# A parallel attention and gated block, forward and backward, on one core: another layout of the weight loads, paired query weights, wider products and a new order

## The chip, the core and the metric

The kernel runs on one core of a Trainium2 chip. A core has five engines with an instruction stream each: TensorE (PE, with PEld for its weight loads), VectorE (DVE), ScalarE (ACT), GpSimd (POOL) and SyncE (SP). Sixteen DMA engines move data between HBM and the core's SBUF; nearly every transfer here is issued from SP. The metric is the device time of one execution in microseconds (us), and lower is better.

## The reference, cut to what matters

The reference takes one decode step for two sequences (B = 2, one query position, D = 576) and returns the output and all eight gradients.

```python
xn = _layernorm(x)                                    # (2, 1, 576)
out = x + A(xn, k_cache, v_cache, wq, wo) + Bm(xn, w_gate, w_up, w_down)

# A: 32 query heads over 16 K/V heads, 4096 cached positions of 128 numbers each
q = (xn @ wq) per head;  k, v = repeat(k_cache, 2), repeat(v_cache, 2)
p = softmax(q @ k.T * 128 ** -0.5);   A = (p @ v) @ wo
# Bm: F = 4608
h = (xn @ w_gate) * (xn @ w_up);      Bm = h @ w_down

out, vjp = jax.vjp(f, x, k_cache, v_cache, wq, wo, w_gate, w_up, w_down)
return out, *vjp(grad_out)
```

Each cache has 2 x 16 heads of 4096 x 128 bf16, 1 MB a head. The gradients of the caches and of the five weight matrices are outer products of a few rows, but they are as large as the tensors themselves: the profile counts 92.48 MB read from HBM and 92.48 MB written.

## The kernel before, in words

The work on the caches is cut into 16 steps `s`. A step has one sequence `b = s % 2` and one group `g = s // 2` of two K/V heads, hence four query heads. A step loads two K heads and two V heads (`load_kv`, L1117, 1 MB each), turns them in 32 x 32 blocks on DVE (`turn`, the helper `t32` at L464), forms scores (`score`, L1234), the softmax, the scores' gradient, the weighted sums (`contract`, L1407), and then the gradients of K and V (`head_outer`, L1255) in PSUM. ACT or DVE (`cp`, L468 and L470) copies those to SBUF, and `put` (L691) stores 1 MB a head.

A group also needs four heads' columns of `wq` and rows of `wo` (`load_w`, L1132 to L1141). `group_front` forms the queries from `wq` (L966) and takes the gradient back through `wo`; `group_back` forms the output's share and the input's gradient, for which it turns the group's `wq` on DVE (L464, tile `ww`). The gated block goes in nine parts of 512 columns of F (`mlp`), loaded two at a time: 1024 columns of `w_gate` and `w_up` (L1155 the first 512 rows, L1158 the last 64, the tail), and two parts of `w_down` (L1164). The gradients of `wq`, `w_gate` and `w_up` are stored for up to four parts at once (`wide_outer`, products at L759), those of the tails apart (`tail_outer`).

How the rows of a weight matrix lie in SBUF matters here. Of the first 512 rows, partition `p` holds rows `p`, `p + 128`, `p + 256` and `p + 384`; the loads and the loops over `dc` in `group_front`, `mlp` and `dxn` follow that.

The order of the work is not written by hand. While the program is built, `Order.run` plays all streams (`turn`, `fronts`, `attend`, `backs` and so on) against a model of engine times, DMA lines and buffers. Priorities come from `pr` and the tables `HEAD`, `TAIL`, `PR`, `OFF`; `MLP_AT`, `WQ_AT`, `WO_AT` say after which K/V load a weight load may go. The instructions of each engine are emitted in that order. SP's DMAs are one such list: a store that waits for its copies holds up each load behind it.

Buffers: `NBIG` = 16 buffers of 1 MB are shared by K/V loads (`kv`, up to 7), turned blocks (`X`), gate and up weights (`G`) and stores (`st`, up to 4); 6 `ww` buffers hold `wq`, `wo` and `w_down`; the gradients that `wide_outer` multiplies lie in 5 tiles `D` and 6 tiles `Q`.

Of the kernel before, what the change touches and what calls it, by code (L numbers as in the profile page):

```python
# [13 lines left out]
P = 128  # L14
# [90 lines left out]
class Order:  # L105
# [3 lines left out]
    def __init__(self):  # L109
        self.free = {e: 0.0 for e in ("PE", "ACT", "DVE", "POOL", "SP")}  # L110
        self.slots = {}
        self.home, self.cap, self.used = {}, {}, {}
        self.lines = Lines()
        self.quad, self.kind = (None, 0.0, 0.0), None
        self.streams = []
        self.count = 0
        self.log = []
        self.lanes = {"HW": [], "SW": []}
# [17 lines left out]
    def advance(self, s, value):  # L136
        while True:
# [13 lines left out]
            elif kind == "spawn":  # L151
                self.spawn(s.req[1], s.req[2], s.ready)
            elif kind == "prio":
                s.prio = (s.req[1], s.prio[1])
            elif kind == "lset":
                s.req[1].t = Late(s.land)
            elif kind == "lrel":
                self.pool(s.req[1])[s.req[2]] = s.land
                if s.req[1] in self.used:
                    self.used[s.req[1]] -= 1  # L160
            else:
                return

# [31 lines left out]
    def run(self):  # L195
        while self.streams:
# [8 lines left out]
            if e is not None:  # L205
                t, _, s, e = min((c for c in cand if c[3] == e and c[0] <= t + SLACK[e]), key=lambda c: (c[1], c[0]))
# [27 lines left out]
            elif r[0] == "dma":  # L234
                self.free[e] = t + r[2]
                s.land = self.lines.push(e == "POOL", t + r[2] + LATENCY[e], r[3], r[4])
# [54 lines left out]
def DMA(engine, cost, nbytes, row=8192):  # L291
# [5 lines left out]
NBIG, NGU, NWW, NBD = 16, 1, 6, 3  # L297
CAP = {"kv": 7, "X": 15, "st": 4, "G": 2}
OFF = {"mload": {0: 96.4, 1: -26.1, 2: 880.0, 3: 94.9, 4: -346.4, 5: -156.4, 6: -87.6, 7: 8.9, 8: 146.0, 9: -13.8,
       10: 91.2, 11: -99.0, 12: -61.7, 13: 103.4, 14: 404.9, 15: -150.5}, "wload": {0: -50.8, 1: -238.8, 3: -315.1,  # L300
# [7 lines left out]
       "load": {0: 195.1, 2: 227.9, 3: -17.9, 4: -185.2, 5: -111.1, 6: -195.0, 7: -157.8, 8: 475.0, 10: 90.3,  # L308
       11: -45.9, 12: -113.2, 13: 340.9, 14: 38.7, 15: -10.9}, "front": {1: -351.4, 2: 56.5, 3: 55.5, 4: 1100.6,
       5: 44.1, 6: -364.2, 7: -8.3, 8: -150.0, 10: 278.3, 11: -217.9, 12: 25.9, 14: -46.2, 15: 809.6},  # L310
       "turn0": {0: -96.0, 1: 186.1, 2: 128.2, 3: 344.6, 4: 259.4, 5: 502.5, 6: 22.0, 7: -80.7, 8: 79.6, 9: -81.7,
       10: -397.2, 11: -241.3, 12: -223.5, 13: -195.7, 14: 186.3, 15: 55.8}, "con": {0: -121.6, 1: 346.9, 2: 7.7,
# [3 lines left out]
       "back": {0: 413.0, 1: -6.1, 2: 233.5, 3: 588.7, 4: 263.1, 5: -92.6, 6: -1063.1, 7: 111.3, 8: 44.4, 10: -315.0,  # L316
# [3 lines left out]
       11: -7.4, 12: 14.8, 13: 23.1, 14: 398.8, 15: -591.6}, "dsc": {0: -130.6, 2: -312.2, 3: -339.0, 4: 207.7,  # L320
       5: -530.4, 6: 41.2, 7: 323.6, 8: -0.4, 9: 644.8, 10: -274.2, 11: 125.7, 12: 309.5, 13: -43.5, 14: 192.2,
       15: -0.7}, "mlp": {0: 81.6, 1: -71.7, 2: 147.3, 3: -224.1, 4: -6.3, 5: 14.7, 6: 616.7, 7: -152.4, 8: -159.9,
       9: 42.7, 10: -45.7, 11: 24.0, 12: 245.6, 13: -6.0, 14: -127.2, 15: -22.4}, "att": {0: 251.8, 1: -520.9,
       2: 62.8, 3: 21.5, 4: -199.3, 5: -366.7, 6: 546.7, 7: -109.6, 8: -638.2, 9: 1.5, 10: -174.3, 11: 113.2,
       12: 18.4, 13: -79.6, 14: -31.8, 15: -12.4}, "conv": {1: 208.9, 2: -233.1, 3: 119.4, 4: 0.3, 5: -102.3,
       6: -60.5, 8: 9.6, 9: -114.9, 10: 102.5, 11: 45.1, 12: 165.0, 13: -36.7, 14: 23.6, 15: -54.5}}
MLP_AT = [1.22, 5.43, 16.39, 14.23, 25.87, 33.08, 39.74, 38.29, 101.55]
WQ_AT = [-2, 5, 9, 22, 32, 30, 50, 47]
WO_AT = [-10, -14, -8, 3, 37, 36, 48, 48]
LATENCY, DRY = {"SP": 0.5, "ACT": 0.5, "POOL": 0.57}, 0.4  # L330
LM, LAG = 0.67, 1.7
CLK = 2.0
BIAS = 0.196
SLACK = {"PE": 0, "ACT": 0.21, "DVE": 0.48, "POOL": 937075237.61, "SP": 6210463039.22}
STEP = 28.0
HEAD = {"turn0": -109.2, "turn1": -1091.6, "att": -224.6, "dsc": -208.3, "con": 390.9, "out1": -1503.4,
        "out0": 772.1, "front": 803.5, "back": -715.7, "W0": 1770.6, "W1": 26.3, "BD1": 1384.3, "BD0": 3893.2,
        "conv": -396.6, "load": 469.8}
TAIL = {"turn0": -167.6, "turn1": 1451.8, "att": -1608.9, "dsc": 1030.3, "con": 1577.7, "conv": 3.8, "out1": 2595.4,
        "out0": -474.0, "front": -576.5, "back": 355.2, "W1": 698.1, "BD1": -2114.1, "BD0": 951.5, "load": 618.9,  # L340
        "W0": 381.9}
PR = {"turn0": 410.8, "turn1": -89.2, "att": -1586.1, "dsc": -1566.9, "conv": 32.7, "con": -332.6, "out1": 2476.3,
      "out0": 866.1, "front": 94.3, "back": -196.2, "W0": -1406.3, "W1": -128.9, "BD1": 1706.7, "BD0": -477.7,
      "mlp": -490.2, "wout": -771.6, "store": -4.6, "load": 401.7, "wload": -1959.2, "fin": -1327.7, "const": 3504.2,
      "mload": -416.2}
# [8 lines left out]
def kernel(  # L354
# [45 lines left out]
    WB = 4 * FS + 256  # L400
# [10 lines left out]
    kv_t = X_t = st_t = G_t = tiles("big", NBIG, [P, NCH * Dh])  # L411
# [4 lines left out]
    tl_t = tiles("tl", 2, [P, FS])  # L416
    BD_t = tiles("BD", NBD, [P, 16, Dh])
# [3 lines left out]
    D_t = tiles("D", 5, [P, 2, P])  # L421
# [12 lines left out]
    Q_t = tiles("Q", 6, [P, P])  # L434
# [125 lines left out]
    Emore, Ein, Eprep = Event(), Event(), Event()  # L560
# [19 lines left out]
    def front_y():  # L580
        yield WAIT(Ein)
# [10 lines left out]

    def front():
        xb, yb = xy[:, 0:D], xy[:, D:2 * D]
        for t, src in ((xb, A_x), (yb, grad_out)):
            yield DMA("ACT", 0.45, 2304, 1152)
            nc.scalar.dma_start(t, src.rearrange("b s d -> (b s) d"))
        yield ("lset", Ein)
        yield SPAWN(front_y(), -999.0)
# [11 lines left out]
        nc.vector.tensor_scalar(xnb[:], xb, mv[:, 0:1], rstd[:], op0=ALU.subtract, op1=ALU.mult)  # L611
# [6 lines left out]
        for c in range(4):  # L618
            nc.tensor.transpose(tp[:, 2 * c:2 * c + 2], xnb[:, c * P:(c + 1) * P], ident[0:2, 0:2])
        nc.tensor.transpose(tp[0:64, 8:10], xnb[:, 512:576], ident[0:2, 0:2])  # L620
        nc.tensor.transpose(tp[:, 10:12], xnb[:, 448:576], ident[0:2, 0:2])
# [3 lines left out]
        nc.vector.tensor_copy(xs[64:128, 5, 0:2], tp[64:128, 10:12])  # L625
        yield REL("m", i)
# [8 lines left out]
        yield DVE(0.3)  # L635
        nc.vector.memset(gg[:, 1], 0.0)
# [6 lines left out]
        for a in range(4):  # L643
            for c in range(4):
                nc.tensor.matmul(tp[32 * c:32 * c + 32, 2 * a:2 * a + 2], lhsT=xb[:, P * c + 32 * a:P * c + 32 * a + 32],
                                 rhs=ident[0:2, 0:2], start=True, stop=True)
        for a in range(2):
            nc.tensor.matmul(tp[0:32, 8 + 2 * a:10 + 2 * a], lhsT=xb[:, 512 + 32 * a:544 + 32 * a],
# [12 lines left out]
    def stationaries(i, rep, npos, half, costs):  # L661
# [6 lines left out]
        for h in range(2):  # L668
# [5 lines left out]
    def dxn(dp, i, X, S, pos, xoff, xstep, Xt, St, toff, tpos):  # L674
# [6 lines left out]
        for s in range(St):  # L681
            for q in range(4):
                nc.tensor.matmul(dp[32 * q:32 * q + 32, P:160], lhsT=view(Wt[:], 0, P, 8 * tpos(q, s), [[1, 32]]),
# [875 lines left out]
```

## Time and profile before

| what | value |
|---|---|
| three timed runs | median 477.73 us (476.86 to 479.79) |
| the profiled execution | 480.7 us, its span 478.9 us |
| mean granted TensorE clock | 0.704 |
| DMA | 185.95 MB in 41925 packets, 388 GB/s over the span |
| issues from SP, 1 MB each | 74 stores, 32 K loads, 32 V loads, 4 gate and 4 up loads |
| `wq` loads | 8 of 512 KB, 16 of 32 KB |

The span runs from the first to the last instruction on the core; the profiled execution's own time lies 1.8 us above it. In the profile's page, part 1 gives the busy time of each engine, part 2 cuts the span into 40 equal slices, part 3 lists the DMA queues, and part 5 the groups of equal instructions with busy time and the mean of one. A window of the DMA view gives, for a stretch in us from the span's start, the packets that the 16 DMA engines moved, the MB, and the time that the packets took as a share of 16 engines' time. The records of neighbouring packets overlap a little, so a share can pass 100%.

### The profile page before, as it was taken

What the parts mean: (1) busy time and instruction counts of PE and PEld (TensorE: products, weight loads), DVE (VectorE), ACT (ScalarE), POOL (GpSimd) and SP (SyncE); (2) the same over time, 40 slices, a digit from 0 to 9 for tenths busy, and PEclk for the clock granted to TensorE, in tenths of its full rate; (3) what the DMA queues carried; (4) which work ended last, traced back from release to release, by engine and by line L of the source; (5) the groups of instructions that cost most, each with busy time, mean ns of one, the idle gap of its engine ahead of it and who ended that gap; (6) DMA issues with size and microseconds to landing.
All of it is one profiled execution on the core that took longest, in us unless ns stands there. A gap on an engine that the chain in (4) does not pass through costs nothing.

```text
span 478.9 us, 15380 instructions
## 1 busy us (share of the span) xinstructions
PE 375.8 (78%) x6538; PEld 214.9 (45%) x6538; DVE 369.2 (77%) x708; ACT 335.6 (70%) x507; POOL 152.0 (32%) x208
## 2 busy tenths in 40 slices
PE   1668588989878877768878986599887769898894
PEld 1545353545554534446344453464444424444452
DVE  8788787867867976786956987889677958888781
ACT  3139659966787693833869875399776978897871
POOL 0440074343003643003434530032644556333000
PEclk9979676556766677885567595859656876656876
DMA  8999999999999999999999999999999999999994
GB/s 299 355 405 419 391 402 380 353 377 422 422 400 371 395 365 393 423 414 389 316 399 384 354 402 422 421 413 406 346 414 415 418 419 422 419 417 391 425 369 187
DMA packets 41925, 185.95 MB, mean 388 GB/s; under 512 B 3960, under 2 KB 13440, under 8 KB 25472
## 3 DMA queue, kind: packets, MB, share of 16 engines
q1 hardware_dynamic: 41848, 184.96, 98.3%
q8 instruction: 51, 0.84, 0.7%
q14 instruction: 18, 0.15, 0.1%
q10 hardware_dynamic: 8, 0.00, 0.0%
HBM read 92.48 MB, written 92.48 MB: 386 GB/s over the span
## 4 chain that ended last, share of the span: by engine, by line
DMA 46%; PE 25%; DVE 14%; ACT 8%; issue 3%; SPq 2%; POOL 1%; DVEq 0%; ACTq 0%; POOLq 0%
DMA out_dram<-big 18%; DMA big<-in_A_v_cache_dram 15%; DVE big L464 8%; ACT big L468 7%; PE ps_o L1255 4%; DMA big<-in_A_k_cache_dram 4%; PE ps_m L1234 4%; PE ps_m L1407 4%; PE ps_o L722 3%; DMA gu<-in_B_w_up_dram 3%; DMA ww<-in_A_wo_dram 3%; DMA big<-in_B_w_gate_dram 2%; DVE big L470 2%; PE ps_m L678 1%; PE ps_o L759 1%
## 5 line engine op out<-in xcount | busy, mean ns | idle before, releaser
L468 ACT CAST big<-ps_o 128x1024 bf16<-128x1024 f32 (+2 forms) x310 | 277.6, 958 | 47.6 <-PE ps_o L1255 18.9
L464 DVE STREAM_TRANSPOSE big<-big 128x1024 f32<-128x1024 f32 x146 | 175.9, 1224 | 29.7 <-DMA out_dram<-big 16.2
L1222 POOL TENSOR_TENSOR BD<-vr,mask 128x2048 bf16<-128x2048 bf16 x32 | 115.3, 3603 | 105.4 <-ACT vr L468 49.8
L470 DVE CAST big<-ps_o 128x1024 bf16<-128x1024 f32 (+2 forms) x68 | 74.2, 1093 | 16.4 <-PE ps_o L722 7.4
L1234 PE MATMUL ps_m<-big,W 128*32 128x128 bf16 x2048 | 59.9, 282 | 11.3 <-DVE cr L1359 2.6
L1234 PEld LDWEIGHTS <-W 128*32 128x32 bf16 x2048 | 46.7, 125 | 27.9 <-issue 25.7
L1255 PE MATMUL ps_o<-BD,dd 32*128 32x512 bf16 x256 | 45.8, 480 | 9.9 <-ACT big L468 7.9
L671 POOL COPY wt<-wm 64x128 bf16<-64x128 bf16 (+1 forms) x34 | 8.9, 261 | 138.2 <-DVE wm L664 119.5
L1255 PE MATMUL ps_o<-BD,pp 32*128 32x512 bf16 x256 | 48.2, 520 | 5.5 <-ACT big L468 4.0
L1199 POOL COPY W<-rep 32x16 bf16<-32x16 bf16 x128 | 24.5, 192 | 55.8 <-DVE rep L983 33.6
L464 DVE STREAM_TRANSPOSE big<-ww 128x1152 f32<-128x1152 f32 x25 | 34.0, 1359 | 7.7 <-DMA ww<-in_B_w_down_dram 3.5
L1407 PE MATMUL ps_m<-big,pp 128*32 128x512 bf16 x256 | 30.2, 547 | 3.8 <-DMA big<-in_A_v_cache_dram 3.3
L1255 PEld LDWEIGHTS <-dd 32*128 32x128 bf16 x256 | 12.2, 98 | 32.1 <-issue 27.6
L1407 PE MATMUL ps_m<-big,dd 128*32 128x512 bf16 x256 | 25.8, 491 | 0.4 <-DVE oT L1427 0.2
L1255 PEld LDWEIGHTS <-pp 32*128 32x128 bf16 x256 | 10.4, 97 | 28.1 <-issue 24.2
L872 PE MATMUL ps_m<-big,Wdy 128*128 128x128 bf16 x162 | 15.4, 269 | 4.8 <-DVE rz L1320 3.1
L722 PE MATMUL ps_o<-dyr,hb 32*32 32x288 bf16 x288 | 18.0, 382 | 0.2 <-ACT big L468 0.2
L759 PEld LDWEIGHTS <-xnr 32*128 32x128 bf16 x368 | 12.9, 116 | 10.8 <-issue 9.7
L722 PE MATMUL ps_o<-dyr,R 32*32 32x288 bf16 x256 | 16.2, 378 | 1.3 <-ACT big L468 0.9
L872 PEld LDWEIGHTS <-Wdy 128*128 128x128 bf16 x162 | 13.6, 121 | 6.8 <-issue 6.7
L759 PE MATMUL ps_o<-D,xnr 32*128 32x128 bf16 x256 | 13.0, 276 | 3.9 <-issue 2.2
L1308 ACT COPY mr<-m 1x128 f32<-1x128 f32 x16 | 4.7, 295 | 15.8 <-DVE m L1306 15.6
(205 smaller groups left out, 487.3 us busy)
## 6 DMA issues: line engine op xcount, KB each, us to landing
out_dram<-big SPq DMA_DIRECT2D x74, 1024.0 KB, 12.8
big<-in_A_k_cache_dram SPq DMA_DIRECT2D x32, 1024.0 KB, 12.7
big<-in_A_v_cache_dram SPq DMA_DIRECT2D x32, 1024.0 KB, 13.2
out_dram<-big SPq DMA_DIRECT2D x17, 576.0 KB, 10.7
ww<-in_B_w_down_dram SPq DMA_DIRECT2D x9, 576.0 KB, 13.5
ww<-in_A_wo_dram SPq DMA_DIRECT2D x8, 576.0 KB, 7.3
ww<-in_A_wq_dram SPq DMA_DIRECT2D x8, 512.0 KB, 8.0
big<-in_B_w_gate_dram SPq DMA_DIRECT2D x4, 1024.0 KB, 12.3
```

Source lines behind the costliest of these rows:

```text
L464: nc.vector.transpose(out, in_)
L468: nc.scalar.copy(out, in_)
L470: nc.vector.tensor_copy(out=out, in_=in_)
L671: nc.gpsimd.tensor_copy(view(Wt[:], 64 * h, 64, 0, [[dims[-1][1], n], [1, dims[-1][1]]]), view(Wm[:], 64 * h, 64, off, dims))
L722: nc.tensor.matmul(o[32 * q:32 * q + 32, aa, 0:HD2], lhsT=view(t, 32 * q, 32, 2 * A + aa, [[4, 32]]), rhs=dyr[32 * q:32 * q + 32, k * HD2: ...
L759: nc.tensor.matmul(o[:, aa, j * P:(j + 1) * P], lhsT=xnr[32 * a:32 * a + 32, dc * P:(dc + 1) * P], rhs=rhs(a), start=True, stop=True)
L872: nc.tensor.matmul(dh, lhsT=Wdy[:, e, 2 * k:2 * k + P], rhs=view(X[:], 0, P, 64 * k + e, [[D, FC], [2, 32]]), start=(k == 0 and e == 0), s ...
L1199: nc.gpsimd.tensor_copy(view(W_t[t][w][:], 32 * a, 32, 6 + 8 * a, [[G * WW, 4], [WW, G], [1, 2]]), view(rep_t[grp[g]["qs"]][:], 32 * a, 32 ...
L1222: nc.gpsimd.tensor_tensor(BD_t[i][:], view(vr_t[v][:], 0, P, 0, [[0, 16], [1, Dh]]), view(mask16[:], 0, P, 0, [[1, 16], [0, Dh]]), ALU.mult)
L1234: nc.tensor.matmul(sc[32 * cq:32 * cq + 32, :], lhsT=view(W[:], 0, P, (be * G + l) * WW + 6 - 4 * c2 - 2 * l, [[1, 32]]), rhs=view(X[:], 0 ...
L1255: nc.tensor.matmul(o[:, k, :], lhsT=pr2[32 * c4:32 * c4 + 32, :], rhs=BD[32 * c4:32 * c4 + 32, 8 * l + 4 * h2:8 * l + 4 * h2 + 4, :], star ...
L1407: nc.tensor.matmul(ct[32 * j:32 * j + 32, :], lhsT=view(rT, 0, P, 4 * c + 2 * l, [[1, 32]]), rhs=kv_t[kvS[s][t][l]][:, Dh * c:Dh * (c + 4) ...
```

## The change

- **Rows.** [...] In the loads of `wq`, `w_gate` and `w_up` the 576 rows are now cut in 16 blocks of 36. The first 32 of block `e` go to partitions `8e` to `8e + 7`, four neighbouring rows to each (`main_rows`); its last four are the tail (`tail_rows`). The rest of the program follows: `xn` is permuted the same way (`by_rows`), and so are the views for `final_dx`.
- **Pairs.** `wq` is loaded for two groups at once, except for groups 0 and 1: 1024 columns instead of 512, into one of the big buffers (`wq`, up to 2 of them), with the tail in two tiles `qt`. A buffer is free when both groups have turned their half. `ww` has 4 buffers instead of 6, `NBIG` is 17.
- **Wide products.** The 4 slots of `D` and of `Q` lie in one tile each, so a product of `wide_outer` takes up to 512 columns at once instead of 128 at a time.
- **grad_out first.** Its load goes from ACT's queue to the first place of SP's list.
- **Order.** The tables are new, `st` may take 9 buffers and `X` 8, `head_outer` and `wide_outer` wait for part of the product before them, and two of the model's constants differ (`LM` 0.24 for 0.67, `LAG` 2.75 for 1.7).

```diff
-NBIG, NGU, NWW, NBD = 16, 1, 6, 3
-CAP = {"kv": 7, "X": 15, "st": 4, "G": 2}
+NBIG, NGU, NWW, NBD = 17, 1, 4, 3
+CAP = {"kv": 7, "X": 8, "st": 9, "G": 2, "wq": 2}
...
-LM, LAG = 0.67, 1.7
+LM, LAG = 0.24, 2.75
...
+    def main_rows(A):
+        return A.rearrange("(e r) n -> e r n", e=16)[:, 0:32, :].rearrange("e (j c) n -> e j c n", c=4)
+
+    def tail_rows(A):
+        return A.rearrange("(e r) n -> e r n", e=16)[:, 32:36, :]
...
             if kind == "wq":
-                for h in range(2):
-                    yield DMA("SP", 0.36, 64 * 256 * 2, 512)
-                    nc.sync.dma_start(ww_t[w][64 * h:64 * h + 64, 4 * FS:WB],
-                                      A_wq[512:576, n0 + 256 * h:n0 + 256 * h + 256])
...
+                js = [j] if i < 2 else [0, 1] if j == 0 else []
+                for k in js:
+                    yield DMA("SP", 0.36, 64 * FS * 2, 1024)
+                    nc.sync.dma_start(t[64 * k:64 * k + 64, :], tail_rows(A_wq[:, n0 + FS * (k - j):n0 + FS * (k - j) + FS]))
+                if js:
...
+                    width = FS * len(js)
+                    yield DMA("SP", 0.4, 128 * 4 * width * 2, 2 * width)
+                    nc.sync.dma_start(w[:].rearrange("p (c n) -> p c n", n=2 * FS)[:, :, FS * js[0]:FS * js[0] + width],
+                                      main_rows(A_wq[:, n0:n0 + width]))
...
-                                  Wsrc[0:512, f0:f0 + width].rearrange("(c p) n -> p c n", p=P))
+                                  main_rows(Wsrc[:, f0:f0 + width]))
...
-                nc.sync.dma_start(gu[64 * w:64 * w + 64, 0:width], Wsrc[512:576, f0:f0 + width])
+                nc.sync.dma_start(gu[64 * w:64 * w + 64, 0:width], tail_rows(Wsrc[:, f0:f0 + width]))
...
-            for j, rhs in enumerate(rhss):
-                for aa in range(2):
-                    a = 2 * A + aa
-                    nc.tensor.matmul(o[:, aa, j * P:(j + 1) * P], lhsT=xnr[32 * a:32 * a + 32, dc * P:(dc + 1) * P],
-                                     rhs=rhs(a), start=True, stop=True)
+            for aa in range(2):
+                a = 2 * A + aa
+                nc.tensor.matmul(o[:, aa, 0:n * P], lhsT=xnr[32 * a:32 * a + 32, dc * P:(dc + 1) * P],
+                                 rhs=rhs(a), start=True, stop=True)
...
-        t32(pairs(X[:, 0:WB]), pairs(wq[:]))
-        yield REL("ww", st["wq"])
+        t32(pairs(X[:, 0:4 * FS]).rearrange("p (c n) -> p c n", c=4),
+            pairs(wq[:]).rearrange("p (c n) -> p c n", c=4)[:, :, HFS * j:HFS * (j + 1)])
+        yield DVE(0.4)
+        t32(pairs(X[64 * j:64 * j + 64, 4 * FS:5 * FS]), pairs(wt[64 * j:64 * j + 64, :]))
...
     def front_y():
-        yield WAIT(Ein)
+        yield DMA("SP", 0.36, 2304, 1152)
+        nc.sync.dma_start(xy[:, D:2 * D], grad_out.rearrange("b s d -> (b s) d"))
...
-            nc.vector.tensor_scalar(xnb[:], xb, mv[:, 0:1], rstd[:], op0=ALU.subtract, op1=ALU.mult)
+        for d, r in by_rows(xp, xb):
+            nc.vector.tensor_scalar(d, r, mv[:, 0:1], rstd[:], op0=ALU.subtract, op1=ALU.mult)
```

More of the change, by code (lines that the diff above doesn't have):

```diff
@@ L115, in __init__ @@
         self.streams = []
+        self.last = None
         self.count = 0
@@ L162, in advance, with again, stores @@
                 return
+    def again(self, s, e):
+        return ALT if e == "SP" and self.stores(s) == self.last else 0.0
+    def stores(self, s):
+        return s.gen.__name__ in ("put", "final_out", "final_dx")
     def start(self, s):
@@ L339 @@
[L339 to L345, printed above, removed]
+ALT = 0.0
@@ L667, in stationaries @@
         yield POOL(costs[1])
-        for h in range(2):
+        for h in hs:
             off, dims = half(h)
@@ L1018, in group_front, with free_wq @@
         yield SET(st["Ed"])
+    def free_wq(pair):
+        yield WAIT(*pair["turned"])
+        yield REL("wq", pair["w"])
+        yield REL("qt", pair["t"])
     def group_back(g):
@@ L1167, in load_w @@
                 yield SPAWN(mlp(k, hh, sl, Lgu, Ld, d), pr("mlp", MLP_AT[k] / 4))
+    wqs = [dict(turned=events(2)) for _ in range(NG // 2)]
     def load_ws(items):
@@ L1473, in final_out @@
                                  start=False, stop=True)
-        yield from rows_put(o, 0, out_0)
+        yield from rows_put(o, 0, out_0, [
+            (view(xy[:], 0, 2, 64 * k, [[P, 5 - k], [1, 64]]),
+             o[0:2, k, 0:320 - 64 * k].rearrange("p (k n) -> p k n", k=5 - k)) for k in range(2)])
         yield REL("o", i)
```

237 lines of the change are left out of this document (139 added, 98 removed), and 23 rows, old and new, of the table OFF.

## The prediction

> **What bounds the kernel now.** I read the page's busy times first, then its DMA queues, then the rates of the DMA by slices, then single windows of the DMA view where the rate is low, and last what SP waits for.
>
> ```profile
> PE 375.8 (78%) x6538; PEld 214.9 (45%) x6538; DVE 369.2 (77%) x708; ACT 335.6 (70%) x507; POOL 152.0 (32%) x208
> ...
> DMA  8999999999999999999999999999999999999994
> GB/s 299 355 405 419 391 402 380 353 377 422 422 400 371 395 365 393 423 414 389 316 399 384 354 402 422 421 413 406 346 414 415 418 419 422 419 417 391 425 369 187
> ...
> q1 hardware_dynamic: 41848, 184.96, 98.3%
> ```
>
> No compute engine is above 78% of the span, while the packets of SP's queue took 98.3% of all 16 DMA engines' time. So the DMA is the bound, and the time changes only through three things: the time that packets take, stretches in which the DMA runs dry, and the ends of the span. The slices show the first: the DMA is busy throughout, but it moves 415 to 425 GB/s in good slices and 316 to 371 in others. Most of the poor ones lie where gate and up weights load (slices 2, 8, 15, 23, 24), or `wq` and `wo` (13, 29), as SP's issue times say. Two neighbouring windows of the first of these stretches, 12 to 14 us and 14 to 16 us:
>
> ```profile
> q1 hardware_dynamic: 407, 0.80, 107.4%
> ```
> ```profile
> q1 hardware_dynamic: 288, 0.57, 104.2%
> ```
>
> Both are nearly all 2 KB rows of the gated block's weights. Without the few packets under 512 B, which take under 1% of the time, the first holds 382 of 2 KB and two of 8 KB, the second 276 of 2 KB. An 8 KB packet takes 313 ns (28 to 30 us: 102 in 100.3%). So a 2 KB packet takes (1.074 x 16 x 2000 - 2 x 313) / 382 = 88 ns in the first window and 33,344 / 276 = 121 ns in the second. The first is `w_gate`'s main load, the second begins with its tail and `w_up`. Slow stretches follow at every pair of parts: 308 GB/s in 14 to 20 us, 325 in 95 to 102, 344 in 174 to 184, 346 in 271 to 279, against 399 in 12 to 14.
>
> **The change, part by part.** The sum is made against the profiled execution's 480.7 us (span 478.9, 1.8 around it), which is 3.0 above the median of 477.73; at the end I take 3.0 off.
>
> *Fewer, larger packets.* Groups 2 to 7 load `wq` in three pairs: 6 x 512 = 3072 packets of 1 KB become 1536 of 2 KB. The last window, 476 to 479 us, has 35 packets of 1 KB and 2 small ones in 3.4% of 48,000 ns, 47 ns each. So this saves (3072 x 47 - 1536 x 88) / 16 = 0.6 us. The tails go from 1024 pieces of 512 B to 512 of 1 KB. No window isolates 512 B; if one costs half of 47 ns nothing is saved, if it costs as much 1.5 us. I take 0.3, near the lower end: from 2 KB to 1 KB a packet's time falls from 88 to 47 ns, nearly by half. Sum -0.9.
>
> *Which rows an engine reads.* If all slow stretches ran like 12 to 14 us, they would give back 6 x (1 - 308/399) = 1.4, 7 x (1 - 325/399) = 1.3, 10 x (1 - 344/399) = 1.4 and 8 x (1 - 346/399) = 1.1 us, 5.2 in all. The two stretches of `wq` and `wo`, 145 to 148 us at 276 GB/s and 345 to 349 at 277, would give 3 x 0.25 + 4 x 0.25 = 1.8 against the 370 GB/s of a mix of 1 KB (349) and 4.6 KB rows. The upper bound is 7.0. The lower bound is below nothing: if the new rows made all 4608 packets of gate and up take 121 ns instead of a mean near 100 (92 to 95 us: 512 in 107.0% of 48,000), it would cost 4608 x 21 / 16 = 6.0. Neither end is excluded: `w_gate`'s main load runs at 88 ns with the old rows, so they aren't slow by themselves; the slowness begins when a second block of rows is read beside it. [...] I take a gain of 4.0, nearer to the row of 12 to 14 us.
>
> [...]
>
> *The end.* In 472 to 476 us the queue's share is 28.1%, in 476 to 479 it is 3.4%, in 468 to 472 88.5%:
>
> ```profile
> q1 hardware_dynamic: 319, 0.39, 28.1%
> ```
> ```profile
> q1 hardware_dynamic: 37, 0.04, 3.4%
> ```
>
> 0.46 + 2.88 + 2.90 = 6.2 us of DMA time are lost. From 473 on the rate is 14 to 31 GB/s in most slices, a sixteenth of 420: one engine works off its backlog of the last stores. In the changed order `out_0`, a 1 MB store, `out_1` and two 1 MB stores come last, 2.5 us each at 421 GB/s; before, `out_1` itself is last and waits for the input gradient's chain until 473.8 us. So that chain gets cover. But 10.8 MB stand behind the last weight load instead of 11.8, the chain is still there, and so may the lagging engine be. Bounds -3.0 and +2.5 (the 1 MB less); I take -1.5.
>
> *The start.* `grad_out` is issued ahead of the first K load, which moves from 0.73 us to about 1.2 us; group 0 issues one tail fewer behind it. Before the first packets nothing hides this: +0.4, at least 0. The two strided passes that replace one pass over `xn` (0.42 us on DVE) come before the first queries; the DMA works on loads already issued, so nothing.
>
> *DVE, PE and POOL.* Each group's `wq` is turned in 1.22 us (the 128x1024 row) and 0.42 us (the 128x256 row) instead of 1.36: 8 x 0.28 = 2.3 us of DVE, hidden under the DMA but for the last group, +0.3. `wide_outer` issues 96 products instead of 368; the columns streamed are the same, so PE keeps its time and the 272 weight loads less (12.9 us for 368) come off PEld, which overlaps PE. The 64 extra small products of the tail rows (12.2 us for 416 of them, so 1.9) are on PE at 78%. None of it is on the path as long as the DMA is the bound; if that cover goes, +2 on DVE and PE each.
>
> *Buffers and order.* SP's waits before:
>
> ```profile
> SPq L691 <- ACT big L468: 82.6, 49, 7.7
> SPq L691 <- DVE big L470: 49.9, 17, 6.8
> SPq L1117 <- DMA out_dram<-big: 31.9, 13, 4.8
> ```
>
> SP sits 31.9 us at K/V loads until a store frees their buffer, yet the DMA runs dry only in few slices: 0.95 in 216 to 228 us, 0.90 in 228 to 240, 0.94 in 252 to 264, 0.95 in 456 to 468, together 3.1 us. After, up to two of 17 big buffers hold `wq`, so 15 to 17 are left for the rest where 16 were; queued behind a load that waits is every store. The four fixed slots of `D` make part 4 wait for the products of parts 0 to 3; in the compiled order their stores (four of 2 x 2048 columns) come ahead of part 4's loads, so that wait is free. The new order may lose up to 3.1 less or some 12 more (the second rival). I take no change.
>
> Sum: 480.7 - 0.9 - 4.0 - 1.5 + 0.4 + 0.3 = 475.0; less 3.0 is **472.0 us**.
>
> **Rivals.** *A: the slow stretches stay.* They begin with the tail. A tail goes to 64 partitions before and after, so if its destination and not its rows brings the engines out of step, the largest term goes: 476.0. For it: the old rows ran at 88 ns. Against it: the 1 KB stores of the end, tails from 64 partitions among them, show 47 ns. [...]
>
> *B: slower, for want of a big buffer.* When a pair of `wq` is loaded while the former is still held (three times: groups 2, 4, 6), a K/V load has to wait for a further 1 MB store to drain, 2.5 us, and everything on SP queues behind it. In 227 to 231 us this shows what a gap costs: share 70.5%, 1.2 us. With the wait and the stage behind it each handover would cost up to 4 us, 12 in all: 484. It decides from about 10 us of dry DMA beyond the present 3.1. Against it: `ww` no longer holds `wq`, and `st` may take 9.
>
> *C: all goes well.* Slow stretches gone (-7.0), the end gains 3.0: 480.7 - 0.9 - 7.0 - 3.0 + 0.7 - 3.0 = 467.5, and with dry stretches gone 464.5.
>
> **How the numbers follow.** Forecast 0.42, C 0.18, A 0.28, B 0.12. What can be told from no change is 1%, so 473.0 is the limit of faster, 482.5 of slower. The forecast's own spread (its end term between -3.0 and +2.5) leaves a fifth of it above 473. Faster 0.42 x 0.8 + 0.18 + a little of A = 0.56; slower most of B, 0.10; same 0.34. The range takes in C with dry stretches gone, the forecast and A with its bad end, 464 to 480; B is left out.
>
> **What would show it.** Gate and up windows at 380 GB/s and more (A: still 310 to 345); some 2050 packets fewer in all; a share above 60% until 3 us before the end; the dry slices no deeper than 0.90 (B: slices at 0.8 after the `wq` pairs' loads). I am wrong if the new rows slow the loads themselves, or if the compute behind the last load, not the DMA, sets the end.

## The result, and the profile after

The changed kernel takes **523.7 us** (median of four runs, 521.6 to 525.9) against 477.3 us of the kernel before beside it: a ratio of 1.096, 95% interval 1.090 to 1.102. It is slower by 46 us, where 472.0 was forecast. The profiled execution has a span of 521.1 us, 42.2 more than before. (In one experiment below, Order alone, one of four runs lies over 1.5% above the fastest and is left out of its median and ratio.)

Of the page of the changed kernel, the busy times, the DMA slices and the queue that answer to those shown of before (and the line that counts packets):

```profile
PE 383.1 (74%) x6330; PEld 214.6 (41%) x6330; DVE 381.0 (73%) x722; ACT 330.3 (63%) x505; POOL 150.5 (29%) x200
...
DMA  8999999999999999999899999999999999999576
GB/s 271 239 420 343 415 289 367 220 417 421 390 373 351 418 421 427 250 348 426 351 310 291 382 420 420 416 323 361 418 352 424 346 401 416 420 404 289 208 252 260
DMA packets 39698, 185.91 MB, mean 357 GB/s; under 512 B 3784, under 2 KB 9680, under 8 KB 23248
...
q1 hardware_dynamic: 39628, 184.96, 96.9%
```

The good slices are as good as before, 415 to 427 GB/s. But the poor ones, which lay at 316 to 371, now lie at 220 to 351, with the DMA as busy as ever. And the last four slices, some 52 us, are new: the DMA moves 208 to 289 GB/s there, and in the last three it is no longer busy.

The same two windows as before, 12 to 14 and 14 to 16 us, from the DMA view of the changed kernel (queue, packets, MB, share):

```profile
DMA packets 226, 0.48 MB, mean 238 GB/s; under 512 B 12, under 2 KB 12, under 8 KB 220
...
q1 hardware_dynamic: 226, 0.48, 105.4%
```
```profile
q1 hardware_dynamic: 216, 0.44, 107.0%
```

Of the 226 packets of the first, 12 are tiny, 6 have 8 KB, and 208 have 2 KB, so a 2 KB packet takes about (1.054 x 32,000 - 6 x 313) / 208 = 153 ns; in the second all have 2 KB, 34,240 / 216 = 159 ns. Before it was 88 and 121. The two windows hold 424 packets of 2 KB, fewer than the 512 of `w_gate`'s main load, whose tail is issued behind it: this is the main load alone.

The end, in the windows of the changed kernel (busy times and counts of the engines, granted clock, DMA share, GB/s):

```profile
468.00:480.00 12.00, 5.58 (x92) 3.65 (x81) 5.85 (x14) 2.46 (x8) 0.00 (x0) 0.50 1.06 304
480.00:492.00 12.00, 10.90 (x159) 5.91 (x157) 8.43 (x18) 7.75 (x10) 1.70 (x1) 0.72 0.53 218
492.00:504.00 12.00, 10.87 (x234) 5.82 (x233) 9.83 (x18) 10.13 (x15) 2.70 (x4) 0.72 0.66 240
504.00:516.00 12.00, 8.95 (x110) 4.47 (x108) 8.20 (x18) 8.39 (x11) 0.00 (x0) 0.78 0.60 230
516.00:521.00 5.00, 0.00 (x0) 0.00 (x0) 0.00 (x0) 0.00 (x0) 0.00 (x0) 0.50 0.76 315
```

and in the chain that ended last (start, us, engine, tile and line):

```profile
466.32 11.06 DMA gu<-in_B_w_up_dram
477.42 0.86 PE ps_m L883 x24
479.02 0.46 DVE dd L480
...
505.17 0.98 PE ps_o L1529 x16
507.31 1.22 DVE big L486
510.39 1.63 PE ps_o L1571 x8
...
514.94 1.01 ACT big L484
```

The chain passes through the tail of the last `w_up` load, for 11 us, until 477.4. From there to the last copy its long pieces are compute, on PE, DVE and ACT, with the DMA at 53 to 66%. The windows from 480 on lose 12 x (0.47 + 0.34 + 0.40) + 5 x 0.24 = 15.7 us of DMA time. Before, the last two windows lost 12 x 0.05 + 11 x 0.56 = 6.8:

```profile
456.00:468.00 12.00, 11.16 (x243) 7.70 (x241) 9.32 (x20) 9.19 (x15) 1.04 (x4) 0.72 0.95 373
468.00:479.00 11.00, 3.90 (x52) 2.19 (x42) 1.97 (x10) 1.43 (x2) 0.00 (x0) 0.66 0.44 162
```

There the last load in the chain, a K load, landed at 402.6 us. All behind it was compute too, but the DMA had enough in its queue to stay busy beside it until about 468.

What SP waits for, in the changed kernel:

```profile
SPq L718 <- DVE big L486: 109.9, 39, 12.8
SPq L718 <- ACT big L484: 96.0, 50, 9.9
SPq L1160 <- DMA out_dram<-big: 16.7, 8, 7.2
```

The waits of stores for their copies grew from 132.5 to 205.9 us; those of K/V loads for a free buffer fell from 31.9 to 16.7.

All packet records together close the account. Their durations, summed and divided by 16 engines, are the first column; the second is the time for which fewer than 16 packets are in flight, in the same unit, and the third that for which more than 16 are, since some records overlap. Both are counted from the first packet, 10.5 to 11.2 us ahead of the span, to the last, which ends 1.2 to 1.4 us ahead of the span's end in most runs. Packets plus dry less overlap is that stretch. The rows below the second are the experiments of the next section.

| kernel | packets, us | dry, us | overlap, us | span, us |
|---|---|---|---|---|
| before | 474.6 | 22.8 | 8.9 | 478.9 |
| after | 508.5 | 33.5 | 11.3 | 521.1 |
| after, old rows | 475.7 | 33.7 | 8.6 | 491.4 |
| before, new rows | 512.9 | 22.4 | 12.4 | 513.5 |
| before, 32 blocks of 18 rows | 471.9 | 22.6 | 9.1 | 475.7 |
| before, 128 blocks of 4 rows | 471.6 | 22.7 | 9.0 | 476.1 |
| before, wide products | 470.2 | 23.6 | 8.9 | 475.5 |
| before, one planner constant | 477.6 | 34.0 | 8.5 | 493.4 |
| before, grad_out first | 477.1 | 43.2 | 8.6 | 498.5 |
| after, old rows and old tables | 474.0 | 30.9 | 8.6 | 487.0 |
| after, old rows, no Order | 474.0 | 48.5 | 8.4 | 504.4 |
| after, old rows, kv 8 | 475.7 | 47.6 | 8.7 | 502.8 |

So the 42.2 us of span are 33.9 us of longer packets and 10.7 us of dry DMA, less 2.4 us of more overlap. The experiments take the two apart.

### The profile page after: what moved, and what is told of

The parts are those of the page before. It is cut to its first block, busy times and chain, and to the rows that moved or that the text cites. A ratio compares the mean times of both kernels' runs of the same rounds, so it can differ in the third digit from the quotient of the medians.

```text
span 521.1 us, 14927 instructions
## 1 busy us (share of the span) xinstructions
PE 383.1 (74%) x6330; PEld 214.6 (41%) x6330; DVE 381.0 (73%) x722; ACT 330.3 (63%) x505; POOL 150.5 (29%) x200
## 4 chain that ended last, share of the span: by engine, by line
DMA 48%; PE 27%; DVE 10%; ACT 8%; SPq 3%; issue 3%; POOL 0%; DVEq 0%; ACTq 0%
DMA big<-in_A_v_cache_dram 20%; DMA out_dram<-big 18%; ACT big L484 7%; DMA gu<-in_B_w_up_dram 6%; DVE big L480 6%; PE ps_o L1315 5%; PE ps_m L1467 4%; PE ps_m L1293 3%; PE ps_o L749 3%; DMA ww<-in_A_wo_dram 3%; SPq L1215 2%; PE ps_m L901 2%; DVE big L486 2%; PE ps_m L1031 2%; PE ps_m L705 1%
## 5 line engine op out<-in xcount | busy, mean ns | idle before, releaser
L484 ACT CAST big<-ps_o 128x1024 bf16<-128x1024 f32 (+2 forms) x296 | 266.2, 959 | 54.7 <-PE ps_o L1315 33.6
L480 DVE STREAM_TRANSPOSE big<-big 128x1024 f32<-128x1024 f32 x154 | 185.9, 1224 | 35.2 <-DMA out_dram<-big 12.1
L486 DVE CAST big<-ps_o 128x1024 bf16<-128x1024 f32 (+1 forms) x82 | 89.8, 1096 | 20.5 <-PE ps_o L749 7.1
L698 POOL COPY wt<-wm 64x128 bf16<-64x128 bf16 x26 | 7.4, 286 | 115.3 <-DVE wm L691 114.8
L1258 POOL COPY W<-rep 32x16 bf16<-32x16 bf16 x128 | 24.6, 193 | 41.1 <-DVE rep L1015 34.6
L1467 PE MATMUL ps_m<-big,dd 128*32 128x512 bf16 x256 | 29.1, 545 | 8.1 <-DVE acc L1098 6.3
L480 DVE STREAM_TRANSPOSE big<-ww 128x1152 f32<-128x1152 f32 x17 | 23.2, 1362 | 5.3 <-DMA out_dram<-big 4.1
L1031 PE MATMUL ps_m<-big,Wdy 128*128 128x128 bf16 x144 | 14.9, 284 | 4.7 <-DVE big L480 4.5
L705 PE MATMUL ps_m<-big,wm 128*32 128x128 bf16 x416 | 12.5, 275 | 7.5 <-DVE Dall L908 5.8
L901 PE MATMUL ps_m<-big,Wdy 128*128 128x128 bf16 x162 | 16.6, 283 | 1.7 <-DVE rz L1380 1.2
L484 ACT CAST tl<-ps_o 128x256 bf16<-128x256 f32 (+1 forms) x26 | 9.4, 375 | 12.6 <-PE ps_o L849 12.1
L484 ACT CAST osb<-ps_m 128x512 bf16<-128x512 f32 x15 | 8.8, 588 | 12.7 <-PE ps_m L1467 12.6
## 6 DMA issues: line engine op xcount, KB each, us to landing
big<-in_A_k_cache_dram SPq DMA_DIRECT2D x32, 1024.0 KB, 12.5
out_dram<-big SPq DMA_DIRECT2D x17, 576.0 KB, 10.7
big<-in_B_w_gate_dram SPq DMA_DIRECT2D x4, 1024.0 KB, 19.4
```

The lines of the kernel that those rows point to most:

```text
L480: nc.vector.transpose(out, in_)
L484: nc.scalar.copy(out, in_)
L486: nc.vector.tensor_copy(out=out, in_=in_)
L705: nc.tensor.matmul(dp[32 * q:32 * q + 32, 0:P], lhsT=view(Wm[:], 0, P, 8 * pos(q, s), [[1, 32]]), rhs=view(X, 0, P, xoff(q, s), [[xstep, 4 ...
L901: nc.tensor.matmul(dh, lhsT=Wdy[:, e, 2 * k:2 * k + P], rhs=view(X[:], 0, P, 64 * k + e, [[D, FC], [2, 32]]), start=(k == 0 and e == 0), s ...
L1031: nc.tensor.matmul(dp, lhsT=Wdy[:, e, 2 * k:2 * k + P], rhs=view(X[:], 0, P, 64 * k + e, [[D, GH], [2, 32]]), start=(k == 0 and e == 0), s ...
```

## The experiments

The expectations name the theories as they stood at the time.

### The rows, undone and alone

The changed kernel with the old rows and everything else as changed (the permuted `xn` and the views for `final_dx` go back with them):

```diff
     def main_rows(A):
-        return A.rearrange("(e r) n -> e r n", e=16)[:, 0:32, :].rearrange("e (j c) n -> e j c n", c=4)
+        return A[0:512, :].rearrange("(c p) n -> p c n", p=P)
...
     def tail_rows(A):
-        return A.rearrange("(e r) n -> e r n", e=16)[:, 32:36, :]
+        return A[512:576, :]
```

> The changed kernel with the old rows: the sources of the wq, gate and up loads are again rows p, p+128, p+256, p+384 and the last 64 rows, and xn and the input gradient are no longer permuted. Pairs, wide products, grad_out first, buffers and the planned order stay as changed. Theory 1 (the new rows slow the loads, and a fixed order passes that on): 2 KB packets return from 161 ns to near 100 and the time to 470 to 480 us, about what the sum of the prediction gives without its row term (476). Theory 2 (the new order or the lack of big buffers dries the DMA): the time stays above 500 us.

Measured: 496.0 us, ratio 1.037 (1.033 to 1.041), between the ranges of the two theories. A 2 KB packet takes 103 ns again, as theory 1 asks. SP issues its transfers in the same order as in the changed kernel. So the rows account for 27.7 us, and 18.5 us more than before stay, which theory 1 does not give. (The profiled runs lie only 12.5 us apart: that of before is 3 us above its median, this one 2.4 below.)

The opposite: the kernel before with `main_rows` and `tail_rows` as the only change.

> The kernel before with only the sources of the wq, gate and up loads changed to the blocks of 36 rows; nothing else is adapted, so its products mix permuted rows, with the same amount of work. Theory 1: 2 KB packets go to about 160 ns: 4608 x 61 / 16 = 17.6 us, wq's 1 KB packets from 50 to 72 ns: 5.6 us, and waits behind late weights on top: 500 to 520 us. Theory 2: within 2% of the kernel before, 470 to 487 us.

Measured: 511.7 us, ratio 1.070 (1.065 to 1.075). In the order of before, which SP keeps here, the rows alone cost 34 us, and no dry time (22.4 us against 22.8): the loads are longer, and the DMA is the bound. In the changed order they cost 27.7, with 32.8 us more of packets instead of 38.4. Of these 38.4 us, 18.5 are 2 KB packets (164 ns each instead of 100) and 8.2 are 1 KB packets; 10.7 fall on rows of 4.6 and 8 KB, whose layout no edit touched. So what moves beside the slow loads slows down as well.

### Which part of the rows

A program of loads alone (one run; line numbers are its own). Each group is eight loads of 1 MB, `wq` seven. Two groups of 128 KB tails at its end are too short to read a rate from.

```diff
+    def old(A):
+        return A[0:512, :].rearrange("(c p) n -> p c n", p=P)
+    def block(A, r):
+        return A[0:16 * r, :].rearrange("(e r) n -> e r n", e=16)[:, 0:32, :].rearrange("e (j c) n -> e j c n", c=4)
+    def neighbours(A):
+        return A[0:512, :].rearrange("(p c) n -> p c n", p=P)
```

> Only loads, 8 (wq: 7) of 1 MB in each of eleven groups with a full stop between, then two groups of eight 128 KB tails; it computes nothing and its outputs hold no result. Groups in order: gate/up with old rows; blocks of 36; 32 neighbouring rows without a gap (source pattern of 512 rows); blocks of 34; every 16th row; K cache contiguous; K cache with a partition pitch of 9 KB, written as 128 pieces; the same with 16 blocks of 72 KB, each one run of 64 KB; wq with old rows, blocks of 36, neighbouring rows; tails old, tails new. Theory 1a (addresses: the pitch of 36 rows between engines): blocks of 36 at about 220 GB/s, blocks of 34 or every 16th row clearly different from it, the two K cache groups of 9 KB and 72 KB pitch alike, near 410. Theory 1b (16 as the first count of the source pattern changes which partitions an engine writes at one time): blocks of 36, blocks of 34, every 16th row and the K cache in 16 blocks all near half rate, 200 to 260 GB/s, all patterns that begin with 128 or 512 at 390 and more. [...]

A window inside each group, in order of time (the last two numbers are DMA share and GB/s): gate and up in the old layout, in 16 blocks of 36, as 128 x 4 neighbouring rows, in 16 blocks of 34, and in 16 sets of every 16th row; the K cache contiguous, as 128 pieces at a pitch of 9 KB, and as 16 pieces of 64 KB with a gap; `wq` in the old layout, in blocks of 36 and as neighbours.

```profile
10.00:22.00 12.00, 0.24 (x4) 0.00 (x0) 1.00 1.05 387
32.00:60.00 28.00, 0.29 (x5) 0.00 (x0) 1.00 1.07 213
70.00:80.00 10.00, 0.24 (x4) 0.00 (x0) 1.00 1.05 387
94.00:120.00 26.00, 0.29 (x5) 0.00 (x0) 1.00 1.07 209
132.00:160.00 28.00, 0.35 (x6) 0.00 (x0) 1.00 1.07 209
172.00:184.00 12.00, 0.29 (x5) 0.00 (x0) 1.00 1.01 422
190.00:202.00 12.00, 0.24 (x4) 0.00 (x0) 1.00 1.02 423
212.00:240.00 28.00, 0.35 (x6) 0.00 (x0) 1.00 1.02 223
248.00:260.00 12.00, 0.29 (x5) 0.00 (x0) 1.00 1.05 387
268.00:292.00 24.00, 0.29 (x5) 0.00 (x0) 1.00 1.07 217
300.00:308.00 8.00, 0.18 (x3) 0.00 (x0) 1.00 1.05 387
```

Each pattern is either at full rate or near half of it. Slow are those, and only those, whose source begins with a count of 16: blocks of 36, of 34, every 16th row, and the K cache in 16 pieces, although its runs are 64 KB long. Neighbouring rows are as fast as distant ones, and `wq`, whose old layout jumps 1 MB, is as fast as gate and up, whose layout does not. The slow patterns read at quite different addresses (blocks, every 16th row, long runs), so the addresses are not what they share. And the DMA share is as full in slow groups (1.02 to 1.07) as in fast ones (1.01 to 1.05), so each packet takes longer: by these lines a 2 KB packet takes 16 x 2048 B x 1.07 / 213 GB/s = 165 ns in blocks of 36, and 16 x 2048 B x 1.05 / 387 GB/s = 89 ns in the old layout.

Then the number of blocks, and loads to half of the partitions (again one run):

```diff
+    def block(A, m):
+        return A.rearrange("(e r) n -> e r n", e=m)[:, 0:512 // m, :].rearrange("e (j c) n -> e j c n", c=4)
+    def half(i, p):
+        return T[i][p:p + 64, 0:rows].rearrange("p (c n) -> p c n", c=4)
```

> Only loads again, 8 in each group, the groups apart by a small VectorE write; everything else of the program is left out. Gate and up weights, 1 MB each, with the 576 rows cut in 16, 32 and 64 blocks (32, 16 and 8 neighbouring rows of a block loaded, pitch 36, 18 and 9 rows); the K cache as 16, 32 and 64 blocks of 8 KB runs with a gap behind each; gate and up in the old layout; then half of it (256 rows, 0.5 MB) to partitions 0 to 63, to 64 to 127, and to both halves in turn. [...] Theory C (a count of 16 costs as such, and only the number of blocks matters): 32 and 64 blocks run at 387 and 420, and 64 partitions at 387. If 32 and 64 blocks stay near 212, any cut into blocks with gaps costs half, but then the K cache's 128 pieces at 9 KB of the earlier run (420) show that gaps alone do not.

Windows inside the groups, in order: gate and up in 16, 32 and 64 blocks; the K cache in 16, 32 and 64; gate and up in the old layout; half of its rows to partitions 0 to 63, to 64 to 127, and to the halves in turn.

```profile
16.00:36.00 20.00, 0.24 (x4) 0.00 (x0) 1.00 1.07 220
46.00:60.00 14.00, 0.29 (x5) 0.00 (x0) 1.00 1.05 387
64.00:80.00 16.00, 0.35 (x6) 0.00 (x0) 1.00 1.05 387
92.00:116.00 24.00, 0.29 (x5) 0.00 (x0) 1.00 1.02 228
128.00:140.00 12.00, 0.28 (x5) 0.00 (x0) 1.00 1.01 421
148.00:160.00 12.00, 0.24 (x4) 0.00 (x0) 1.00 1.01 421
168.00:178.00 10.00, 0.24 (x4) 0.00 (x0) 1.00 1.05 386
186.00:204.00 18.00, 0.41 (x7) 0.00 (x0) 1.00 1.07 204
206.00:222.00 16.00, 0.35 (x6) 0.00 (x0) 1.00 1.07 205
226.00:234.00 8.00, 0.24 (x4) 0.00 (x0) 1.00 1.07 231
```

Only 16 blocks are slow; 32 and 64 run at 387 and 421. So blocks with gaps are harmless too. And loads to 64 partitions run near half rate as well (204 and 205 GB/s, and 231 to the halves in turn, against 386), where theory C, a price of the count as such, has 387. So a count of 16 is not the only thing that halves the rate. What it has in common with a destination of 64 partitions is not shown, nor that it changes which partitions an engine writes at one time, as theory 1b has it: no run here records which engine writes which partition.

Last, inside the kernel: the kernel before with 32 blocks of 18 rows, 16 to four partitions each and two for the tail (the first lines below are the edit against the run with blocks of 36), and with 128 blocks of 4, the tail at its old place.

```diff
     def main_rows(A):
-        return A.rearrange("(e r) n -> e r n", e=16)[:, 0:32, :].rearrange("e (j c) n -> e j c n", c=4)
+        return A.rearrange("(e r) n -> e r n", e=32)[:, 0:16, :].rearrange("e (j c) n -> e j c n", c=4)
```

> The kernel before with only the sources of the wq, gate and up loads changed, as in the run of the rows in blocks of 36, but with 32 blocks of 18 rows: 16 neighbouring rows of a block to four partitions, the last two its part of the tail. Everything else is left as before, so the results belong to permuted rows. [...] Should blocks with a gap cost something of their own between other traffic, or the tail beside them: 485 to 512.

```diff
+    def main_rows(A):
+        return A[0:512, :].rearrange("(p c) n -> p c n", p=P)
...
-                                  Wsrc[0:512, f0:f0 + width].rearrange("(c p) n -> p c n", p=P))
+                                  main_rows(Wsrc[:, f0:f0 + width]))
```

> The kernel before with neighbouring rows in the form that ran at full rate alone: partition p holds rows 4p to 4p+3 of the first 512, the tail is the last 64 rows as before; xn and the input gradient are permuted to match. Order as before. If neighbouring rows cure the slow stretches, 2 KB packets go from 100 to 84 to 88 ns and the time falls by 3 to 7 us, 471 to 475. If the stretches come from elsewhere (the tails, or two loads out of step), it stays within 1% of the kernel before; 32 neighbouring rows are certainly no reason for 160 ns: then the time would be above 500.

Measured: 478.8 us for blocks of 18, ratio 1.002 (0.999 to 1.005), and 478.2 us for 128 blocks of 4, ratio 1.000 (0.998 to 1.003). The count of 16 is the whole 34 us. And the gain that was hoped for from neighbouring rows is nothing, inside 0.3%.

### The 18 us that stay

First the planner's part and the limits, in the changed kernel with old rows. With the tables, gates and constants of before (its own limits kept; besides the two constants that the list of the change names, `BIAS` and the planner's `SLACK` differ as well):

```diff
-MLP_AT = [1.69, 6.77, 13.62, 20.7, 30.44, 73.88, 16.24, 56.8, 110.3]
+MLP_AT = [1.22, 5.43, 16.39, 14.23, 25.87, 33.08, 39.74, 38.29, 101.55]
...
-BIAS = 0.091
+BIAS = 0.196
```

> The first experiment (changed kernel, old rows) with the tables and constants of the order from the kernel before (priorities, positions of the weight loads, LM, LAG and the like); pairs, wide products, grad_out first and the buffer counts stay as changed. Its compiled order has 14.5 MB of transfers behind the last V load, where the kernel before has 15.0 and the changed one 12.5. Theory E (what is left, about 18 us, comes from the order, above all from an end with too little to move while the last step's chain runs): most of it goes, 478 to 487 us. Theory S (it comes from the structure: pairs in big buffers, wide products, more turning): it stays at 490 to 500.

With its own tables and eight K/V buffers, so that the last V load goes out earlier (18.6 MB stand behind it in the compiled order, against 12.5 of after and 15.0 of before):

```diff
-CAP = {"kv": 7, "X": 8, "st": 9, "G": 2, "wq": 2}
+CAP = {"kv": 8, "X": 8, "st": 9, "G": 2, "wq": 2}
```

> The first experiment with one number changed: K/V loads may hold 8 of the big buffers instead of 7. The planner then puts the last V load ahead of 18.6 MB of transfers instead of 12.5 (44 us at 421 GB/s against 30 us; the chain from that load's landing to the end took 48 us). Theory E: the DMA no longer runs dry in the last 50 us, which cost 15 us there against 7 in the kernel before: 480 to 488 us. Theory S: within 1% of 496.

Measured: 490.1 us with the old tables, ratio 1.027 (1.021 to 1.033), and 506.4 us with eight buffers, ratio 1.059 (1.054 to 1.064). The second did what it was to do at the end, where about 9 us of dry time went, but a new dry stretch of some 18 us opened between 276 and 312 us, and the sum is worse. From 273 us on SP stood there at three stores for 24.3 us, 17.4 of them in a single wait for a copy. So the end was where the loss lay, not what made it: theory E falls. Theory S is missed as well, which had this run within 1% of 496. The old tables brought back 6 of the 18.5 us, less than E asked for and at the edge of what a price of the structure alone would give.

Then each side of the change alone. Wide products on the kernel before, with every engine's order kept (144 products instead of 368):

```diff
-            for j, rhs in enumerate(rhss):
-                for aa in range(2):
-                    a = 2 * A + aa
-                    nc.tensor.matmul(o[:, aa, j * P:(j + 1) * P], lhsT=xnr[32 * a:32 * a + 32, dc * P:(dc + 1) * P],
-                                     rhs=rhs(a), start=True, stop=True)
+            for aa in range(2):
+                a = 2 * A + aa
+                for j, m, r in rhs:
+                    nc.tensor.matmul(o[:, aa, j * P:(j + m) * P], lhsT=xnr[32 * a:32 * a + 32, dc * P:(dc + 1) * P],
+                                     rhs=r(a), start=True, stop=True)
```

> The kernel before with wide products alone: the slots of D and Q lie in one tile each, and a product of wide_outer takes all neighbouring slots of a bunch at once (144 products instead of 368); each engine's order is unchanged. Theory S (the new structure costs the 18.5 us that stay with the old rows): a wider product holds the PE and its PSUM buffer longer in one piece, so some loss, 480 to 486. Theory O (the order costs them) and theory I (every order is fitted to its structure): no change, 476 to 479, since the same columns are streamed.

The part called Order alone, on the structure of before:

```diff
-CAP = {"kv": 7, "X": 15, "st": 4, "G": 2}
+CAP = {"kv": 7, "X": 8, "st": 9, "G": 2}
...
-    def head_outer(s, t, l, pr2, done):
+    def head_outer(s, t, l, pr2, done, after):
+        yield WAIT(*after)
```

> The kernel before with the part called Order alone: the new tables, the new limits for st (9) and X (8), the model's new constants and the two added waits, with the old rows, single loads of wq, 16 big buffers and narrow products. In the compiled order 12.5 MB stand behind the last V load, as in the changed kernel (before 15.0). Theory O: the loss is here, 490 to 500. Theory S: 474 to 482. Theory I: 488 to 500 as well, but then the next run is slow too.

And everything but Order and the rows, on the changed kernel with old rows and the old tables:

```diff
-CAP = {"kv": 7, "X": 8, "st": 9, "G": 2, "wq": 2}
+CAP = {"kv": 7, "X": 15, "st": 4, "G": 2, "wq": 2}
...
-            yield WAIT(*last[1:2])
...
-        yield WAIT(*after)
```

> The changed kernel with the old rows and the whole part called Order undone (old tables, limits for st and X and constants, no added waits), so pairs, wide products, grad_out first and 17 big buffers alone. 16.6 MB stand behind the last V load in the compiled order. Theory O: 474 to 482. Theory S: 488 to 498. Theory I: 485 to 498 though the order alone is slow as well.

Measured: wide products 476.9 us, ratio 0.997 (0.996 to 0.999); Order alone 489.9 us (485.9 to 492.8), ratio 1.024 (1.017 to 1.032); all but Order 506.3 us, ratio 1.059 (1.056 to 1.062). Order alone costs time, and without it the structure is slower still. That points to theory I, each order is fitted to its program, though 506 lies above the range that this theory gave. If it holds, a small edit after which the planner chooses anew must cost as much, whatever the edit is. Two such, the smallest part of the change and one constant of the planner:

```diff
-        for t, src in ((xb, A_x), (yb, grad_out)):
-            yield DMA("ACT", 0.45, 2304, 1152)
-            nc.scalar.dma_start(t, src.rearrange("b s d -> (b s) d"))
...
+        yield DMA("SP", 0.36, 2304, 1152)
+        nc.sync.dma_start(xy[:, D:2 * D], grad_out.rearrange("b s d -> (b s) d"))
```

> The kernel before with grad_out first alone: its load is the first on SP's list instead of the second on ACT's, and the planner finds its order anew with the old tables; rows, loads of wq, products, buffers and limits as before. 15.25 MB stand behind the last V load (before 15.0). Theory I (tables belong to the program that they were fitted to, and any change of the program that makes the planner choose anew loses that): 483 to 500, with a DMA that is dry for 5 us or more beyond that of before. Theory S (each part of the new structure has a price of its own, and this one has none beyond the start): 477 to 480.

```diff
-BIAS = 0.196
+BIAS = 0.18
```

> The kernel before with one constant of the planner changed, BIAS 0.18 for 0.196; nothing of the program's work differs, but the planner chooses otherwise from some point on (SP's list is the same up to its 82nd row of 235). Theory I: 481 to 500 by the order alone. Theory S: 476 to 480, since no part of the change is in it.

Measured: grad_out first 498.1 us, ratio 1.043 (1.038 to 1.048); one constant 494.1 us, ratio **1.033 (1.028 to 1.039)**. The last is the plainest run of the study. `BIAS` is what the planner adds to the cost of a copy on DVE before it chooses between DVE and ACT; the program's work does not change, only which engine takes some copies, and what follows in the order. It costs 16 us. What SP waits for in that run:

```profile
SPq L691 <- ACT big L468: 98.5, 59, 8.2
SPq L691 <- DVE big L470: 92.7, 36, 10.7
SPq L1117 <- DMA out_dram<-big: 15.2, 9, 4.1
```

These are nearly the waits of the changed kernel: 191.2 us at stores for their copies (after 205.9, before 132.5), 15.2 at K/V loads for a buffer (after 16.7, before 31.9). A store stands at the head of SP's list while its copies are late, and the loads behind it stand too. But this is not the whole mechanism: with grad_out first the same waits are 135.8 and 31.5 us, nearly as before, and the DMA is dry for 43.2 us all the same. What makes it dry there stays open. Two windows of the run with one constant show that the dry DMA does not lie at the end alone:

```profile
240.00:252.00 12.00, 8.04 (x98) 3.23 (x87) 6.88 (x16) 8.13 (x14) 0.00 (x0) 0.72 0.76 317
456.00:468.00 12.00, 11.21 (x165) 6.23 (x155) 8.71 (x16) 8.30 (x13) 2.71 (x1) 0.68 0.63 261
```

Six programs that the planner ordered anew, with tables kept from another program or with one limit or constant changed, took 490 to 506 us. The changed kernel with old rows, 496, lies among them, although its tables came with it. So a price of planning anew is shown, 16 us for one constant, and it is nearly as large as the 18.5 us; that it is all of them is argued. Nor was it run apart which part of a new plan costs: the order, or the engine of each copy. DVE takes 80 of the copies of `big` with the one constant changed, 78 with grad_out first and 82 in the changed kernel, against 68 before. The pairs of `wq` were not run apart with the order kept, so a share of theirs is not excluded, and whether a better order exists for the structure stays open: no run searched for one. Where the order was kept, other rows at full rate and wider products stayed within 0.3% of before.

## Why the prediction was wrong

**What bounds the kernel** was read rightly: the DMA, by packets, dry stretches and ends. Where the order was kept, longer packets came out in the span nearly in full (38.4 us more of them in the run of the new rows alone, 34.6 of span, 3.4 gone in overlap). But of the three large terms of the sum two had the wrong sign.

**"Which rows an engine reads", -4.0 (bounds -7.0 to +6.0).** This is the step that failed most: +28 us in the changed order, +34 in the old one. Two things were wrong. The gain rested on a story about addresses, that slowness "begins when a second block of rows is read beside it"; the runs with neighbouring rows at full rate show no gain at all. No run shows the 4.0 us: in blocks of 36 the rows alone cost 34, in 32 blocks of 18 they left the time at a ratio of 1.002, in 128 blocks of 4 at 1.000. And the lower bound took the slowest 2 KB row of the trace, 121 ns, for the worst that could come. It came from loads whose source begins with a count of 128 or, in the tail, 64. The change put 16 there, which no row of the trace had, and a 2 KB packet now takes some 155 ns, as the two windows show. The bound had also left out `wq`, whose pairs were counted at 88 ns. What had to be priced was not which rows are read but the shape of the source pattern, its first count of 16; the diff showed it plainly. Nor did the sum have a term for the other rows that slow down beside these loads.

**Rival A** laid the slow stretches to the tails, which go to 64 partitions, and left the main loads at their rate. The halves of 64 partitions do run at half rate (204 and 205 GB/s, against 386), so this is a likely cause of the slow stretches behind the tails of before; that they slow the main loads beside them was not tried apart. But the loss came in the main loads, whose 2 KB packets took 153 and 159 ns. The jump of 1 MB in `wq`'s old layout has no part here: alone it runs at 387 GB/s, the same as gate and up.

**"Fewer, larger packets", -0.9.** The count was right, 2227 packets fewer. The gain is too small to be seen: at each size's mean duration before (512 B 28 ns, 1 KB 50, 2 KB 100) it is 0.4 us of DMA time, and with the old rows all packets together took 1.1 us more.

**"The end", -1.5 (bounds -3.0 to +2.5).** Wrong: about +9 (15.7 us lost from 480 on, against 6.8 before). I counted what stands behind the last weight load, as if it were ready to be moved. What sets the end is the compute behind the last loads: the tail of `w_up` lands at 477.4, 44 us of compute follow, and the stores left wait for their copies, so that they fill the DMA for only some 60% of the 41 us from 480 on. The prediction's last sentence had named both ways to be wrong, and both came.

**"Buffers and order", 0.** Wrong by the dry time outside the end, 1.8 us by the profile (10.7 less 8.9), and, more than that, as a judgement. I looked for a want of buffers (rival B) and found cover for it. B has the right sign and came near in size, 12 us from some 10 us of dry DMA, and 10.7 us more were measured; but its mechanism is not what the trace shows, since SP waits less for buffers than before (16.7 us against 31.9). That an order planned anew loses its fit was not among the rivals. The run with one constant shows 16 us for that alone.

**The small terms held.** The first K load was issued at 1.16 us instead of 0.73 (+0.4 was taken). The turns of DVE grew by 2.6 us (2.3). Wider products cost nothing (the 96 of `wide_outer` took 17.9 us of PE, the 368 before 19.4) and gave 0.3% where the order was kept.

## What to carry to other kernels

When a load is reshaped, write down the source pattern that the transfer will carry, its first count above all (16 ran at 209 to 220 GB/s here, 32, 64 and 128 at 386 to 387), and measure that pattern alone before arguing about addresses. When an order is found by a planner with fitted tables, any edit that makes it choose anew has a price of its own, here 2 to 6%: keep the order to measure the edit, and change an unrelated constant to learn the price. A bound taken from the slowest row of the trace holds only for the forms that the trace has.

## What the runs showed of the hardware

- A load to 128 partitions whose source begins with a count of 16 ran at 209 to 220 GB/s with rows of 2 KB and at 223 to 228 with 64 KB runs; with 32, 64 or 128 the same bytes ran at 386 to 387 and at 421 to 423.
- A load to 64 partitions ran at 204 to 205 GB/s, and at 231 when successive loads took the two halves in turn.
- The pitch of rows (8 or 9 KB), neighbouring or distant rows, and gaps between blocks made no difference to the full rate (386 to 387 GB/s with rows of 2 KB).
- Beside loads with a first count of 16, packets of other transfers took longer as well: in the run of the new rows alone, those of 4.6 KB 221 ns instead of 197 (208 in the changed kernel).

The best version found is the kernel before with wide products, 476.9 us, by 0.3%.
